# Chunk 0 of a fused state-space and gated-MLP block: all gate steps before all up steps, loads reordered over three queues, a head that goes tile by tile

## The chip, the cores and the metric

The kernel runs on one core of one Trainium2 chip. A core has five instruction streams that run side by side and wait for each other only through semaphores: TensorE (PE, matrix products into the PSUM banks), VectorE (DVE), ScalarE (ACT), GpSimd (POOL) and SyncE (SP, which here only issues transfers). SP, ACT and POOL can issue DMA transfers; each stream works strictly in its own order, so an instruction that waits holds up everything behind it on that engine. The metric is the time of one execution on the device in microseconds (us), lower is better.

## The reference

```python
x  = A_x                       # 1 x 2048 x 448, bf16
xn = layernorm(x)              # mean and variance over the 448 features, eps 1e-5
# branch A: a diagonal complex recurrence with 448 states
Lam_bar = exp(exp(log_dt) * (Lambda_re + 1j*Lambda_im))
Bu      = xn @ (((Lam_bar - 1) / Lam)[:, None] * Bmat).T
h[t]    = Lam_bar * h[t-1] + Bu[t]                 # over 2048 positions
s       = 2 * real(h @ Cmat.T) + xn * Dskip
# branch B: a gated MLP with 1792 hidden units
b       = (sigmoid(xn @ w_gate) * (xn @ w_up)) @ w_down
out     = x + s * silu(b)
```

## The kernel before

**Tiling.** The 2048 positions are 16 tiles of 128 rows, in four chunks of 512 positions. A chunk needs `xnT`, the normalized rows transposed (features on the partitions). Its gate product and its up product each consist of seven steps m = 0 to 6; a step (`gu_mm`, L607 and L608) makes two groups of 128 hidden units for 512 positions with 7 pairs of matmuls on the two halves of the array, into one of three PSUM slots `gu`. ACT or DVE empties the slot (`gu_evac`). In chunk 0 ACT writes tanh of the gate (L622) and DVE combines it with the up slot straight from PSUM into `hF` (L631); in the later chunks ACT empties both slots (L625 with the sigmoid, L635 a copy) and DVE multiplies (L636). The recurrence of a chunk takes `b_units` (PE, L657 to L673), then `ssm_pair` and `ssm_stack` (DVE, the scans at L724 and L756), which leave `hT`. `down` (L785) multiplies `hF` with the third weight `wd`; `yout` (L813) multiplies `hT` with the scaled C matrix and leaves the output tile.

**The order.** Every operation is given to a planner (`Plan`) with an assumed cost, its inputs and its outputs. PE's order is the order of the calls. For the other engines `solve` computes backwards by when an operation is due, then goes forward in time and always takes the ready operation that is due first; `emit` writes the program in that order, engine by engine. From then on the order is fixed. If an assumed cost is too low, an engine meets an instruction whose input isn't there yet and waits with all that stands behind it.

**The head (chunk 0's `xnT`).** For tiles 0 to 3: `stats` (DVE, L347 and L348), `chain` (the reciprocal standard deviation: DVE L358, L359, a power on POOL L361, a reciprocal on DVE L363), `norm` (DVE, L375 and L379), `pe_transpose` (seven PE transposes L404, then a copy on ACT L406 and one on DVE L408). `warm_mm` runs 5 and then 6 idle matmuls (L341). The order on PE is: transposes of tiles 0 and 1, first halves (256 positions) of gate 0 and up 0, transposes of tiles 2 and 3, first half of gate 1, then the second halves of the three. Then `columns` turns four parameter rows into columns (L436 on POOL, L442 on PE), `tables` makes the sine and cosine tables (DVE L476 to L484, ACT L488 to L504) and `coeffs` the coefficients (POOL).

**Later tiles.** For chunks 1 to 3, `chain` runs on POOL alone, two tiles at a time, in six operations (L358, L359, L361, L364, L367, L369), each planned at 0.35 us. `norm` is then on ACT (L382) and `dma_transpose` (L306) makes `xnT` with two transposing transfers per tile from SP.

**The loads.** SP and ACT issue all of them (`load`, L288): the rows of x, the gate and up weights in halves (partitions 0 to 63 and 64 to 127) and blocks of m = 0-1, 2-3, 4-6, the parameter rows, and on ACT at the end `wd` and the last eight tiles of x. The B and C matrices come by transposing transfers on SP (`b_load`, `c_load`).

Of the kernel before, what the change touches and what calls it, by code (L numbers as in the profile page):

```python
# [18 lines left out]
D = 448  # L19
F = 1792  # L20
P = 128
# [51 lines left out]
class Plan:  # L73
# [53 lines left out]
    def solve(self, pe_from):  # L127
# [55 lines left out]
def kernel(  # L183
# [78 lines left out]
    veb, varb = sbt("veb", [NT, 1]), sbt("varb", [NT, 1])  # L262
# [32 lines left out]
    BLK = [(0, 2), (2, 4), (4, 7)]  # L295
# [9 lines left out]
    def tload(keys, o, i, nbytes, r=(), chain=True):  # L305
        add("SP", 1.2, lambda: Q.dma_start_transpose(out=o, in_=i), r=r, w=keys, dma=nbytes * 2, chain=chain)  # L306
# [43 lines left out]
    def chain(t0, n):  # L350
        e, en, c = (V, "DVE", 0.08) if t0 < TPC else (G, "POOL", 0.35)
        ts = range(t0, t0 + n)
        var, mean = mv[:, t0:t0 + n, 1:2], mv[:, t0:t0 + n, 0:1]
        sd, rs, nm = sdb[:, t0:t0 + n, :], rsd[:, t0:t0 + n, :], nmr[:, t0:t0 + n, :]
        ve = veb[:, t0:t0 + n, :]
        bc = lambda t: t[:].unsqueeze(1).to_broadcast((P, n, 1))
        vb = varb[:, t0:t0 + n, :]
        add(en, c, lambda: e.tensor_copy(out=vb, in_=var), r=[("mv", t) for t in ts], w=[("vb", t) for t in ts])  # L358
        add(en, c, lambda: e.tensor_single_scalar(out=ve, in_=vb, scalar=EPS, op=ALU.add),  # L359
            r=[("vb", t) for t in ts], w=[("ve", t) for t in ts])  # L360
        add("POOL", 0.35, lambda: G.tensor_tensor(out=sd, in0=ve, in1=bc(halfc), op=ALU.pow),  # L361
            r=[("ve", t) for t in ts] + ["consts"], w=[("sd", t) for t in ts])
        add(en, c, (lambda: V.reciprocal(out=rs, in_=sd)) if t0 < TPC else  # L363
            (lambda: G.tensor_tensor(out=rs, in0=sd, in1=bc(negc), op=ALU.pow)),  # L364
            r=[("sd", t) for t in ts] + ["consts"], w=[("rs", t) for t in ts])
        if t0 >= TPC:
            add(en, c, lambda: e.tensor_tensor(out=nm, in0=mean, in1=rs, op=ALU.mult),  # L367
                r=[("mv", t) for t in ts] + [("rs", t) for t in ts], w=[("nm", t) for t in ts])
            add(en, c, lambda: e.tensor_single_scalar(out=nm, in_=nm, scalar=-1.0, op=ALU.mult),  # L369
                r=[("nm", t) for t in ts], w=[("nm", t) for t in ts])  # L370

    def norm(t):
        b = t % NXN
        if t < TPC:
            add("DVE", 0.25, lambda: V.tensor_scalar(out=xn[b][:, 0:448], in0=x_all[:, t, :],  # L375
                                                     scalar1=mv[:, t, 0:1], scalar2=rsd[:, t, :],
                                                     op0=ALU.subtract, op1=ALU.mult),
                r=[("x", t), ("mv", t), ("rs", t)], w=[("xn", b)])
            add("DVE", 0.085, lambda: V.tensor_copy(out=xn[b][:, 448:512], in_=xn[b][:, 0:64]),  # L379
                r=[("xn", b)], w=[("xnw", b)])  # L380
        else:
            add("ACT", 0.6, lambda: A.activation(xn[b][:, 0:448], x_all[:, t, :], ACT.Identity,  # L382
# [15 lines left out]
    def pe_transpose(t):  # L398
# [3 lines left out]
        def f():  # L402
# [5 lines left out]
        add("DVE", 0.467, lambda: V.tensor_copy(out=xnT[0][:, 4:7, js], in_=tp[:, 4:7, :]),  # L408
            r=[("acc", a), ("xnT", 0, t, "a")] if False else [("acc", a)], w=[("xnT", 0, t, "b")])

    def dma_transpose(t):
# [4 lines left out]
        tload([k + ("a",)], xnT[c % 3][:, 0:7:2, js], xn[b][:], P * 1024, r=[("xn", b), ("xnw", b)] + al, chain=c == 1)  # L416
        tload([k + ("b",)], xnT[c % 3][:, 1:6:2, js], xn[b][:, 64:448], P * 768, r=[("xn", b)] + al, chain=c == 1)
# [15 lines left out]
    def columns():  # L433
# [28 lines left out]
        for i in range(4):  # L462
# [3 lines left out]
                 ["ident", "pv", "diag"], ["diag"], 0.4)  # L466
# [3 lines left out]
    def tables():  # L470
        turn = C("turn")
        add("ACT", 1.3, lambda: A.preload_act_table_set("silu_and_others"), r=["r", "dt"], w=["silutab"])
        for pt in range(4):
            vk, nk = ("v", pt), ("nu", pt)
            v, nu = v_t[:, pt, :], nu_t[:, pt, :]
            add("DVE", 0.344, lambda v=v, pt=pt: V.tensor_scalar(out=v, in0=iota[:, 0:NTAB], scalar1=turn[:, pt:pt + 1],  # L476
                                                                 scalar2=None, op0=ALU.mult),
                r=[("wv", 0), "turn"], w=[vk])
            add("DVE", 0.344, lambda v=v, nu=nu: V.tensor_single_scalar(out=nu, in_=v, scalar=MAGIC, op=ALU.add),
# [29 lines left out]
        gate([("vrow", q) for q in range(4)] + ["vroww"], [("hF", 1, m) for m in range(7)])  # L509

    def coeffs():
        def ops(o, x, y, op):
            add("POOL", 0.3, lambda: G.tensor_tensor(out=C(o)[:], in0=val(x), in1=val(y), op=op), r=[x, y], w=[o])
# [4 lines left out]
        def one_(o, x, s, op):  # L518
            add("POOL", 0.3, lambda: G.tensor_single_scalar(out=C(o)[:], in_=val(x), scalar=s, op=op), r=[x], w=[o])
# [475 lines left out]
```

## Time and profile before

| | |
|---|---|
| time before, median of 2 runs | 222.81 us (222.48 to 223.13) |
| the profiled execution's own time | 222.76 us |
| its span in the profile | 222.0 us |
| PE busy | 189.1 us (85%) |
| DVE busy | 160.2 us (72%) |
| ACT busy | 112.6 us (51%) |
| POOL busy | 42.6 us (19%) |
| mean granted PE clock | 0.946 |

The span is what the profile shows of one execution; about 0.8 us of the execution's own time lie outside it. Rows of the timeline view give the start, the duration, the engine and source line, output and inputs, how many instructions are merged in the row, and in brackets how long the engine had stood idle before and who released it. "SPq" and "ACTq" are the issues of transfers on those engines. In the view by stretches a row gives a stretch, its length, the busy time of each engine, the granted PE clock as a share of full speed, the busy share of the DMA engines (queued packets overlap, so it can pass 1) and GB/s.

### The profile page before, as it was taken

Reading aid. Unit: us, or ns where it says so; the run is one execution under the profiler, and the core shown is the slowest. Engines: PE = TensorE matmul, PEld = TensorE weight load, DVE = VectorE, ACT = ScalarE, POOL = GpSimd, SP = SyncE. Lnnn points to the kernel's source line nnn. Section 1 sums busy time; section 2 is a strip of 40 time slices with the busy share of each in tenths; the row PEclk is TensorE's granted clock in tenths of the full one; section 3 lists DMA queues with packets and bytes.
Section 4 is the critical chain, followed back from the end, with each engine's and each line's share of the span. In section 5 each row is a group of like instructions: output and inputs, shape, how many; then the busy total and the mean of one; then the engine's idle time right before and its main releaser. Section 6 shows DMA issues by size and latency. Waiting matters only on the chain.

```text
span 222.0 us, 3617 instructions
## 1 busy us (share of the span) xinstructions
PE 189.1 (85%) x1409; PEld 92.5 (42%) x1416; DVE 160.2 (72%) x301; ACT 112.6 (51%) x155; POOL 42.6 (19%) x97
## 2 busy tenths in 40 slices
PE   7200999999899999196999299999999999999993
PEld 2100664344344444043554144444444544455552
DVE  1501677999999999389999688996169799733144
ACT  0004168498999951651952664653655657430330
POOL 4200168621700029500008520000000000000000
PEclk9755699999999999979999769999999999999998
DMA  6999954470000000142001142000000000101002
GB/s 146 213 235 291 355 128 86 84 163 6 1 0 0 3 0 0 25 84 59 1 24 41 28 96 65 0 21 0 24 0 21 3 0 1 44 22 41 3 15 69
DMA packets 30922, 13.32 MB, mean 60 GB/s; under 512 B 19636, under 2 KB 30904, under 8 KB 30904
## 3 DMA queue, kind: packets, MB, share of 16 engines
q1 hardware_dynamic: 25264, 8.95, 17.7%
q10 hardware_dynamic: 5640, 4.13, 7.0%
q8 instruction: 11, 0.18, 0.3%
q14 instruction: 7, 0.06, 0.1%
HBM read 6.66 MB, written 1.84 MB: 38 GB/s over the span
## 4 chain that ended last, share of the span: by engine, by line
PE 47%; DVE 25%; DMA 9%; POOL 8%; ACT 5%; issue 3%; SPq 0%; ACTq 0%; DVEq 0%; POOLq 0%
PE gu L607 17%; PE acc L785 10%; PE acc L813 7%; DMA wG<-in_B_w_gate_dram 5%; PE gu L785 5%; DMA wU<-in_B_w_up_dram 4%; PE gu L670 4%; DVE wv L724 3%; DVE hF L631 3%; POOL sdb L361 2%; POOL rsd L364 2%; DVE bst L347 2%; DVE hF L636 2%; ACT ub L635 2%; DVE hT L741 1%
## 5 line engine op out<-in xcount | busy, mean ns | idle before, releaser
L607 PE MATMUL gu<-xnT,wG 64*128 64x512 bf16 (+1 forms) x210 | 48.1, 367 | 15.4 <-DMA wU<-in_B_w_up_dram 13.0
L607 PE MATMUL gu<-xnT,wU 64*128 64x512 bf16 (+1 forms) x203 | 49.3, 382 | 4.7 <-ACT sig L625 4.7
L608 PE MATMUL gu<-xnT,wU 64*128 64x512 bf16 (+1 forms) x203 | 49.3, 383 | 0.0
L608 PE MATMUL gu<-xnT,wG 64*128 64x512 bf16 (+1 forms) x210 | 48.2, 367 | 0.0
L785 PE MATMUL acc<-wd,hF 128*128 128x448 bf16 x168 | 34.6, 359 | 0.0
L785 PEld LDWEIGHTS <-hF 128*128 128x128 bf16 x224 | 21.8, 99 | 22.4 <-issue 3.6
L607 PEld LDWEIGHTS <-wG 64*128 64x128 bf16 x210 | 19.4, 95 | 24.5 <-issue 4.4
L607 PEld LDWEIGHTS <-wU 64*128 64x128 bf16 x203 | 19.2, 97 | 23.4 <-issue 3.1
L625 ACT ACTIVATE sig<-gu 128x1024 bf16<-128x1024 f32 x21 | 21.5, 1022 | 14.6 <-PE gu L608 14.6
L635 ACT CAST ub<-gu 128x1024 bf16<-128x1024 f32 x21 | 21.2, 1010 | 13.8 <-PE gu L608 13.7
L636 DVE TENSOR_TENSOR hF<-sig,ub 128x1024 bf16<-128x1024 bf16 x21 | 14.3, 682 | 14.9 <-ACT ub L635 14.8
L608 PEld LDWEIGHTS <-wG 64*128 64x128 bf16 x210 | 19.2, 95 | 13.9 <-issue 13.9
L813 PE MATMUL acc<-cT,hT 128*128 128x448 bf16 x105 | 24.3, 353 | 0.0
L724 DVE TENSOR_TENSOR_SCAN wv<-c_r,st,z 128x512 bf16<-128x512 f32 x18 | 22.9, 1280 | 0.2
L608 PEld LDWEIGHTS <-wU 64*128 64x128 bf16 x203 | 19.2, 97 | 5.0 <-issue 5.0
L670 PE MATMUL gu<-xnT,bT 128*128 128x512 bf16 x65 | 16.4, 399 | 1.3 <-issue 1.3
L795 DVE TENSOR_TENSOR g_t<-zb,sigd 128x448 bf16<-128x448 bf16 x16 | 6.2, 384 | 15.1 <-ACT zb L794 15.1
L793 ACT ACTIVATE sigd<-acc 128x448 bf16<-128x448 f32 x12 | 6.5, 541 | 15.1 <-PE acc L785 15.0
L681 ACT CAST bus<-gu 128x1024 bf16<-128x1024 f32 x12 | 12.0, 1006 | 3.9 <-PE gu L670 3.9
L382 ACT ACTIVATE xn<-x_all,nmr,rsd 128x448 bf16<-128x448 bf16 x12 | 8.4, 751 | 10.2 <-POOL nmr L369 10.2
L813 PEld LDWEIGHTS <-hT 128*128 128x128 bf16 x119 | 10.4, 98 | 7.3 <-issue 0.4
L347 DVE BATCH_NORM_STATS2 bst<-x_all 128x6 f32<-128x448 bf16 x16 | 9.4, 612 | 4.6 <-DMA x_all<-in_A_x_dram 4.6
(133 smaller groups left out, 275.9 us busy)
## 6 DMA issues: line engine op xcount, KB each, us to landing
out_dram<-o_t SPq DMA_DIRECT2D x15, 112.0 KB, 1.7
wd<-in_B_w_down_dram ACTq DMA_DIRECT2D x1, 1568.0 KB, 15.5
x_all<-in_A_x_dram ACTq DMA_DIRECT2D x1, 896.0 KB
wG<-in_B_w_gate_dram ACTq DMA_DIRECT2D x2, 224.0 KB, 4.4
wU<-in_B_w_up_dram ACTq DMA_DIRECT2D x2, 224.0 KB, 4.7
wG<-in_B_w_gate_dram SPq DMA_DIRECT2D x2, 224.0 KB, 5.6
wU<-in_B_w_up_dram SPq DMA_DIRECT2D x2, 224.0 KB, 5.9
x_all<-in_A_x_dram SPq DMA_DIRECT2D x1, 448.0 KB, 6.4
```

The lines of the kernel that those rows point to most:

```text
L347: add("DVE", 0.53, lambda: V.bn_stats(out=bst[b][:], in_=x_all[:, t, :]), r=[("x", t)], w=[("bst", b)])
L382: add("ACT", 0.6, lambda: A.activation(xn[b][:, 0:448], x_all[:, t, :], ACT.Identity, bias=nmr[:, t, :], scale=rsd[:, t, :]), r=[("x", t), ...
L607: T.matmul(gu[a][:, 0, ts], lhsT=w_[0:H, s, ms], rhs=x[0:H, s, ts], start=(s == 0), stop=(s == 6))
L608: T.matmul(gu[a][:, 1, ts], lhsT=w_[H:P, (s + 1) % 7, ms], rhs=x[H:P, s, ts], start=(s == 0), stop=(s == 6))
L625: add("ACT", act(1024), lambda: A.activation(sig[b][:], gu[a][:], ACT.Sigmoid), r=[("gu", a), "sinL", "cosL", "sth", "cth"] + [(s, p) for ...
L635: add("ACT", act(1024), lambda: A.copy(out=ub[b][:], in_=gu[a][:]), r=[("gu", a)], w=[("ub", b)])
L636: add("DVE", dve2(1024), lambda: V.tensor_tensor(out=ho, in0=sig[sb_][:], in1=ub[b][:], op=ALU.mult), r=[("sig", sb_), ("ub", b)], w=hk)
L670: T.matmul(gu[a][:, i, :], lhsT=bT[:, kt, i, pt * P:pt * P + P], rhs=x[:, 2 * kt, :], start=False, stop=(kt == 2))
L681: add("ACT", act(1024), lambda u=u, a=a: A.copy(out=bus[u][:], in_=gu[a][:]), r=[("gu", a)], w=[("bus", u)])
L724: dve(1.194, lambda k=k: V.tensor_tensor_scan(out=wv[:, k, :], data0=rb, data1=z[:, k, :], initial=(st[pt][:, k, :] if c else 0.0), op0=AL ...
L785: T.matmul(d, lhsT=hF[c % 2][:, m, h, js], rhs=wd[:, ft, :], start=(ft == 0), stop=(ft == FT - 1))
L813: T.matmul(y, lhsT=hT[c % 2][:, hm, js], rhs=cT[:, cm, c0:c1], start=(i == 0), stop=(i == 6))
```

## The change

**Order of chunk 0.** PE makes all seven gate steps, then all seven up steps; the tanh of gate m waits in `hF` of chunk 1, which is free until then, instead of a ring of two buffers. Ten full steps now precede the two `b_units` of chunk 0 and one follows them; before it was seven and four. The parameter rows move from the memory of the second `hF` to that of the first.

**Loads.** Weight blocks are m = 0-2 and 3-6. SP and ACT load x tiles 0 to 3, then all gate weights, then all up weights; ACT issues only three of these. The parameter rows, `wd` and the last eight tiles of x are issued by POOL. x tiles 4 to 7 come last among SP's plain loads.

**Head.** Each of tiles 0 to 3 has its own chain: DVE adds eps, ACT takes the square root (a table set for it is loaded first), DVE copies the mean and takes the reciprocal. `mv` becomes bf16, so the chains of the later tiles lose one POOL operation. Twelve warm-up matmuls come first. PE's order is: transpose of tile 0, gate steps 0 to 2 for tile 0's 128 positions, transpose of tile 1, the same three steps for tile 1, transposes of tiles 2 and 3, `columns`, then the three steps for tiles 2 and 3.

**Planner.** Its assumed costs change (the POOL operations of a chain from 0.35 to 0.4 or 1.0 us, among others), and an operation that hands over to another engine is due 0.2 us earlier, a transfer 1.5 us instead of 0.5.

```diff
-                if o.dma:
-                    x -= 0.5
+                if kind is not None and o.eng != b.eng:
+                    x -= 1.5 if o.dma else 0.2
...
-    vrow = hF_raw[1][0:1, 0:2048].rearrange("p (a b) -> p a b", a=4)
-    mv = sbt("mv", [NT, 2], FP32)
+    vrow = hF_raw[0][0:1, 0:2048].rearrange("p (a b) -> p a b", a=4)
+    mv = sbt("mv", [NT, 2])
+    meanf = sbt("meanf", [TPC, 1], FP32)
...
-    BLK = [(0, 2), (2, 4), (4, 7)]
+    BLK = [(0, 3), (3, 7)]
...
+    add("ACT", 1.3, lambda: A.preload_act_table_set("sqrt_and_others"), w=["sqrttab"], chain=True)
     load_x(0, 1)
     load_x(1, 1)
+    load_x(2, 2)
     load_w("ACT", "g", 1, 0)
     load_w("SP", "g", 0, 0)
+    load_w("ACT", "g", 1, 1)
+    load_w("SP", "g", 0, 1)
     load_w("ACT", "u", 1, 0)
-    load_x(2, 2)
     load_w("SP", "u", 0, 0)
+    load_w("SP", "u", 1, 1)
+    load_w("SP", "u", 0, 1)
     for k, vec in enumerate((A_log_dt, A_Lambda_im, A_Lambda_re, A_Dskip)):
-        load("ACT", ("vrow", k), D * 2, vrow[:, k, 0:448], vec.unsqueeze(0))
-    for b in (1, 2):
-        if b == 2:
-            load_x(4, 4)
-        for k in ("g", "u"):
-            load_w("SP", k, 0, b)
-            load_w("ACT", k, 1, b)
+        load("POOL", ("vrow", k), D * 2, vrow[:, k, 0:448], vec.unsqueeze(0), cost=1.0)
...
+        if t0 < TPC:
+            add("DVE", 0.09, lambda: V.tensor_single_scalar(out=ve, in_=var, scalar=EPS, op=ALU.add), r=ks("mv"), w=ks("ve"))
+            add("ACT", 0.2, lambda: A.activation(sd, ve, ACT.Sqrt), r=ks("ve") + ["sqrttab"], w=ks("sd"))
+            add("DVE", 0.09, lambda: V.tensor_copy(out=meanf[:, t0:t0 + n, :], in_=mean), r=ks("mv"), w=ks("mf"))
+            add("DVE", 0.09, lambda: V.reciprocal(out=rs, in_=sd), r=ks("sd"), w=ks("rs"))
+            return
...
+        add("POOL", 0.4, lambda: G.tensor_single_scalar(out=ve, in_=var, scalar=EPS, op=ALU.add), r=ks("mv"), w=ks("ve"))
+        add("POOL", 1.0, lambda: G.tensor_tensor(out=sd, in0=ve, in1=bc(halfc), op=ALU.pow), r=ks("ve") + ["consts"], w=ks("sd"))
+        add("POOL", 1.0, lambda: G.tensor_tensor(out=rs, in0=sd, in1=bc(negc), op=ALU.pow), r=ks("sd") + ["consts"], w=ks("rs"))
+        add("POOL", 0.4, lambda: G.tensor_tensor(out=nm, in0=mean, in1=rs, op=ALU.mult), r=ks("mv") + ks("rs"), w=ks("nm"))
+        add("POOL", 0.4, lambda: G.tensor_single_scalar(out=nm, in_=nm, scalar=-1.0, op=ALU.mult), r=ks("nm"), w=ks("nm"))
...
-                add("ACT", act(1024), lambda: A.activation(sig[b][:], gu[a][:], ACT.Tanh, scale=0.5),
-                    r=[("gu", a)], w=[("sig", b)])
+                add("ACT", act(1024), lambda: A.activation(th, gu[a][:], ACT.Tanh, scale=0.5),
+                    r=[("gu", a)], w=[("hF", 1, m)])
...
-        m, k = i // 2, "gu"[i % 2]
+        m, k = (i // 2, "gu"[i % 2]) if c else (i % 7, "gu"[i // 7])
...
-    warm_mm(5)
+    warm_mm(12)
     for t in range(4):
         stats(t)
...
+        chain(t, 1)
+        norm(t)
+    slots0 = [next_gu() for _ in range(3)]
...
     pe_transpose(0)
+    g_head(0, 1)
     pe_transpose(1)
...
+    g_head(1, 2)
     pe_transpose(2)
     pe_transpose(3)
...
     columns()
+    for m in range(3):
+        gu_mm(0, "g", m, slots0[m], 2, 4, m == 0)
+        gu_evac(0, "g", m, slots0[m])
     tables()
     coeffs()
+    load_x(4, 4)
     b_load()
-    load("ACT", "wd", F * D * 2, wd[:], B_w_down.rearrange("(ft p) d -> p ft d", p=P))
-    load_x(8, 8, "ACT")
+    load("POOL", "wd", F * D * 2, wd[:], B_w_down.rearrange("(ft p) d -> p ft d", p=P), cost=1.0)
+    load_x(8, 8, "POOL")
...
-    for i in range(3, 10):
+    for i in range(3, 13):
         gu_step(0, i)
     b_units(0, (0, 1))
     b_units(0, (2, 3))
-    for i in range(10, 14):
-        gu_step(0, i, i == 10)
+    for i in range(13, 14):
+        gu_step(0, i, i == 13)
```

More of the change, by code (lines that the diff above doesn't have):

```diff
@@ L359, in chain @@
[L359 to L370, printed above, removed]
+        sd, rs, nm, ve = (q[:, t0:t0 + n, :] for q in (sdb, rsd, nmr, veb))
+        ks = lambda k: [(k, t) for t in ts]
+        if t0 < TPC:
[4 more added lines that the diff above has]
+            return
@@ L407, in pe_transpose @@
             r=[("acc", a)], w=[("xnT", 0, t, "a")])
[L408 to L409 removed]
+        add("DVE", 0.27, lambda: V.tensor_copy(out=xnT[0][:, 4:7, js], in_=tp[:, 4:7, :]),
+            r=[("acc", a)], w=[("xnT", 0, t, "b")])
     def dma_transpose(t):
```

64 lines of the change are left out of this document (24 added, 40 removed).

## The prediction, made before the changed kernel was run

> **What bounds the kernel now.** I read the page's strip of 40 slices first (5.55 us each), for where PE, which is 85% busy, has holes.
>
> ```profile
> PE   7200999999899999196999299999999999999993
> PEclk9755699999999999979999769999999999999998
> ```
>
> There are three: slices 1 to 3 in the head, slice 16 and its neighbour, slice 22. Elsewhere PE is full, and from slice 23 on it sets the pace to the end. The view by stretches gives each hole its size.
>
> ```profile
> 8.90:21.95 13.05, 0.01 (x1) 0.04 (x1) 0.51 (x3) 2.36 (x3) 0.39 (x1) 0.50 1.14 251
> 53.70:89.80 36.10, 35.24 (x267) 16.19 (x266) 35.45 (x62) 25.98 (x38) 13.43 (x23) 1.00 0.00 1
> 89.80:104.50 14.70, 8.35 (x47) 3.63 (x48) 9.88 (x19) 7.43 (x10) 2.01 (x7) 0.88 0.30 64
> 122.20:131.70 9.50, 5.59 (x18) 2.67 (x19) 6.80 (x11) 7.05 (x10) 4.38 (x9) 0.64 0.27 58
> ```
>
> After the stretch come PE, PEld, DVE, ACT and POOL, the granted clock, the DMA share, GB/s. The head loses 13.0 us. The second hole loses 14.70 - 8.35 = 6.4 us idle, and at a mean clock of 0.88 another 0.12 x 14.70 = 1.8: 8.1 together. The third loses 3.9 idle and, with the 0.36 missing from the clock less a half microsecond that fell on idle time, about 2.9: 6.8. The last two make 14.9 us. Now the causes, from the timeline. First the head:
>
> ```profile
> 8.34 0.57 PE L404 MATMUL acc<-ident,xn 128*128 128x128 bf16 x7 [0.15 <-DVE xn L375]
> 10.83 0.63 ACTq L288 DMA_DIRECT2D wd<-in_B_w_down_dram  x1
> 19.11 0.40 ACTq L288 DMA_DIRECT2D x_all<-in_A_x_dram  x1
> 19.54 1.28 ACT L406 ACT_TABLE_LOAD   x1 [19.54 <-DMA wU<-in_B_w_up_dram]
> 20.83 1.07 ACT L406 COPY xnT<-acc 128x512 bf16<-128x512 bf16 x2
> 21.95 0.37 PE L607 MATMUL gu<-xnT,wG 64*128 64x256 bf16 x1 [13.04 <-DMA wU<-in_B_w_up_dram]
> ```
>
> The bracket on PE names a weight, but the rows above it tell another story: the transposes of tiles 0 and 1 were in PSUM at 8.9, and ACT, which must copy them out, was stuck in its own queue. It issued `wd` at 10.83 and the second half of x only at 19.11, when an up weight had landed; then came its table load, then the copies. PE starts as the second copy ends (21.90). **The head's bound is ACT's queue.** Then the other two holes:
>
> ```profile
> 81.70 0.92 POOL L358 CAST varb<-mv 128x2 bf16<-128x2 f32 x2 [21.55 <-DVE mv L348]
> 90.16 0.79 POOL L369 TENSOR_SCALAR nmr<-nmr 128x2 f32<-128x2 f32 x2
> 90.80 2.71 ACT L382 ACTIVATE xn<-x_all,nmr,rsd 128x448 bf16<-128x448 bf16 x4 [6.18 <-POOL nmr L369]
> 94.47 0.58 PE L607 MATMUL gu<-xnT,wU 64*128 64x512 bf16 x1 [4.70 <-ACT sig L625]
> 102.98 0.37 PE L607 MATMUL gu<-xnT,wG 64*128 64x512 bf16 x1 [1.06 <-DMA xnT<-xn]
> 117.30 0.99 POOL L358 CAST varb<-mv 128x2 bf16<-128x2 f32 x2 [23.49 <-DVE mv L348]
> 123.80 0.41 POOL L369 TENSOR_SCALAR nmr<-nmr 128x2 f32<-128x2 f32 x2
> 124.07 0.76 ACT L382 ACTIVATE xn<-x_all,nmr,rsd 128x448 bf16<-128x448 bf16 x1 [4.07 <-POOL nmr L369]
> 125.78 0.37 PE L660 MATMUL gu<-xnT,bT 64*128 64x256 bf16 x1 [3.60 <-ACT ub L635]
> ```
>
> Both are one mechanism. POOL's chain for two pairs of tiles took 9.2 us (81.70 to 90.95) and 6.9 (117.30 to 124.21); the planner had put it down as 12 x 0.35 = 4.2. ACT meets the norms too early, stands 6.18 and 4.07 us, and behind the norms stand the evacuations that PE waits for.
>
> **The change, part by part. Head.** The rows for its terms:
>
> ```profile
> 0.00:8.90 8.90, 5.66 (x25) 2.33 (x26) 3.83 (x15) 0.00 (x0) 3.48 (x15) 0.99 0.85 174
> 1.30 4.54 PE L341 MATMUL gu<-warm 128*128 128x512 bf16 x11 [1.30 <-POOL warm L309]
> 2.87 0.63 DVE L347 BATCH_NORM_STATS2 bst<-x_all 128x6 f32<-128x448 bf16 x1 [2.87 <-DMA x_all<-in_A_x_dram]
> 21.45 0.85 DVE L408 COPY xnT<-acc 128x384 bf16<-128x384 bf16 x2 [12.41 <-ACT xnT L406]
> 25.06 1.31 PE L404 MATMUL acc<-ident,xn 128*128 128x128 bf16 x14
> 26.01 0.59 ACT L406 COPY xnT<-acc 128x512 bf16<-128x512 bf16 x1 [4.11 <-PE acc L404]
> 27.92 0.27 PE L607 MATMUL gu<-xnT,wG 64*128 64x256 bf16 x1 [0.69 <-ACT xnT L406]
> 28.90 1.02 ACT L622 ACTIVATE sig<-gu 128x1024 bf16<-128x1024 f32 x1 [1.03 <-PE gu L608]
> 29.96 1.22 DVE L631 SCALAR_TENSOR_TENSOR hF<-sig,gu 128x1024 bf16<-128x1024 bf16 x1 [0.92 <-ACT sig L622]
> 30.80 0.39 PE L607 MATMUL gu<-xnT,wU 64*128 64x512 bf16 x1
> ```
>
> Warm-up: 12 x 0.41 from 1.30 ends at 6.3. Tile 0 lands at 2.87; its statistics (0.63) and seven short operations, one of them now on ACT, may take until 6.3 without being seen. The transpose goes at 6.3, and with 0.57, a copy of 0.59 on ACT and 0.43 on DVE behind it `xnT` of tile 0 is there at 7.9. The first gate block needs 448 KB of x and 2 x 336 KB of weights before it: 1.15 MB at the 174 GB/s of the first 8.9 us, 6.6 us, and a good microsecond to complete: 8.0. So gate steps for tile 0 start at **8.0**. Three steps on 128 positions are 21 pairs; the trace has no such matmul. From below: half of a 256-position pair at full clock, 2.3 us for 21 pairs from 27.92 on, so 1.2. From above: that pair at half clock, 0.213 each, 4.5. I take 2.6, since a 128-column transpose with its load takes 0.094 (1.31 for 14) and a pair has two loads. Then 0.57 for the transpose of tile 1, 1.1 for its two copies, 2.6 for the next quarter, 1.31 for the transposes of tiles 2 and 3, 1.4 until their copies are out (`columns`, 16 matmuls of one column, lies in that), and 2.3 for the second halves: 8.0 + 2.6 + 0.57 + 1.1 + 2.6 + 1.31 + 1.4 + 2.3 = 19.9. Ahead of the first tanh ACT must now load another table, because the square root took the first; gate 0 is done at 18.4, 1.28 + 1.02 later its slot is free: first full step at **20.8**, against 30.80. **The head gives 10.0 us** (5 to 13 with both ends of the quarters and a clock that may be low).
>
> [...]
>
> **POOL's transfers.** No POOL issue is in the trace. From below: the same two loads cost ACT 0.63 and 0.40. From above: the 8.7 us that ACT spent between the start of the one and the end of the other. I take 1 us each for all six (nearest: the issue rows). POOL has nothing else before the copy for `columns`, wanted at about 16, so up to 8 us are hidden. `wd` is wanted when PE starts `down`, tens of microseconds later.
>
> **Tiles 4 to 7 load last.**
>
> ```profile
> 13.98 6.80 SPq L306 DMA_TRANSPOSE bT<-in_A_B_re_dram  x2
> 20.83 6.05 SPq L306 DMA_TRANSPOSE bT<-in_A_B_im_dram  x2
> 32.69 10.82 SPq L306 DMA_TRANSPOSE xnT<-xn  x8
> xnT<-xn SPq DMA_TRANSPOSE x24, 2.4
> 41.93 0.39 PE L657 MATMUL gu<-xnT,bT 64*128 64x512 bf16 x1 [0.38 <-DVE bT L552]
> 47.66 0.39 PE L607 MATMUL gu<-xnT,wG 64*128 64x512 bf16 x1
> 53.71 0.38 PE L607 MATMUL gu<-xnT,wG 64*128 64x512 bf16 x1
> ```
>
> Four full steps take 53.71 - 47.66, so 1.51 each, and `b_units` 5.73. Chunk 1 starts at 20.8 + 10 x 1.51 + 5.73 + 1.51 = 43.1 (before: 53.71) and needs all eight transposes, 10.8 us of SP and 2.4 to land. SP carries 2.98 MB up to those tiles, ACT 1.15, and POOL's 2.5 MB share the engines, half or all of them ahead: 5.4 to 6.7 MB. With 1.55 moved by 8.9 us and 251 GB/s after, tiles 4 to 7 land at 24 to 29; statistics (0.63), a pair's chain (half of 6.9, less the dropped cast, 3.0), a norm (0.76) and 13.2 make 42 to 47. So a new wait of 0 to 4 us on PE, with SP's transposes as its cause; I charge **1.0**. The four transposes of B stand on SP between those loads and chunk 1's transposes; issued while the DMA engines were full they held SP 12.9 us (13.98 to 26.88). Now they can follow the last x load from about 10 us on and end at 23 to 28, no later than the tiles are ready, and `b_units` wants them at 36.
>
> **Evacuations.** Ten steps in a row: the gate's tanh 1.02 on ACT, then the up step's 1.22 on DVE, each under 1.51, so three slots suffice. DVE's tables and statistics ahead of the scans are what they were, but six evacuations come before the scans instead of five, 1.22 us more. That has cover:
>
> ```profile
> 76.81 1.39 DVE L585 SCALAR_TENSOR_TENSOR cT<-xnT,c_sa,ctmp 64x448 bf16<-64x448 bf16 x2
> 83.45 0.35 PE L813 MATMUL acc<-cT,hT 128*128 128x448 bf16 x1
> ```
>
> What the first `yout` needs was ready at 78.2, 5.2 us early. Without that cover it would cost the 1.2.
>
> **The two later holes.** The plan now books a pair's chain at 3.2 us, two at 6.4; measured less the dropped cast they would be 8.3 and 5.9. The planner's error falls from 5.0 to 1.9 and from 2.7 to nothing. Taken off PE's idle 4.70 and 3.60 that leaves 1.8 and 0.9, too short to lose the clock (the wait of 1.06 at 103 left it at full), and of 14.9 us some 12 would go. But the whole order is new and DVE, 35.45 of 36.10 busy ahead of the second hole, has no room for statistics that come late. From nothing to 14.9, I take **9.0**.
>
> Sum, on the profiled execution's 222.76: - 10.0 + 1.0 - 9.0 = 204.8, so **205 us**; the median, 222.81, is the same.
>
> **The rivals.** (1) *The holes stay*, because DVE again reaches the statistics late: 222.8 - 9 = 214. For it: it is a new order with the same full DVE. Against: the booked costs. (2) *Both holes close and nothing new waits*: 222.8 - 10 - 14 = 199. (3) *The late tiles bind*: the wait at chunk 1 is 4 to 6 us, PE's clock drops, 1.7 more; with the holes half closed 209, with them open 217. (4) *The change doesn't do what it says*: the first gate steps wait for weights as the bracket at 21.95 says. Then the head gives at most 3 and the time is 211 to 220. Against: 174 GB/s bring the block by 8. [...]
>
> [...]
>
> **How the numbers follow.** Forecast 0.50 (201 to 209), (1) 0.19, (2) 0.12, (3) 0.08, (4) 0.06, (5) 0.05. The range takes in (1), (2) and most of (3): 197 to 216. About 2% is what a measurement here can tell from no change. Faster by more than that: all of 0.50, 0.19, 0.12, 0.07 of (3), 0.03 of (4), together 0.91; within 2%: 0.05; slower: 0.04, the far end of (5).
>
> **What would show it.** In the timeline after: gate matmuls near 8.0 with ACT copies at 7; a full 512-position step near 20.8; chunk 1's first gate step at 43 to 45, and whether a transposing transfer is its releaser; ACT's idle before L382 at 2 us or less and no half-clock stretch past 30 us. The forecast is wrong if POOL is still issuing when `columns` is due, if tiles 4 to 7 land past 29, or if ACT again stands before L382.

## The result and the profile after

The changed kernel takes **206.22 us** (205.85 to 206.59), the kernel before 222.81: a ratio of 0.926 with the interval 0.916 to 0.935. The forecast was 205 (197 to 216). Two kernels among the experiments also had slower executions: one took 208.02 once and 212.65 to 214.11 three times, so it has no ratio and only its head is read, and the last one took 212.45 once in six, which its ratio leaves out.

The strips of the profile after (span 204.8 us, slices of 5.12 us):

```profile
PE   7267995899799999999699999999999999999992
PEclk9859999999999999999999999999999999999998
GB/s 143 235 295 338 223 165 88 74 91 109 89 2 3 0 22 71 78 12 3 73 40 45 48 67 0 3 22 22 0 16 10 0 3 22 22 27 48 0 22 67
```

The clock is at full from slice 3 (15.4 us) to the last but one; before, it fell again in slices 17, 22 and 23. The timeline of PE shows what is left of the holes:

```profile
7.05 0.56 PE L400 MATMUL acc<-ident,xn 128*128 128x128 bf16 x7 [1.18 <-DVE xn L371]
11.68 0.28 PE L603 MATMUL gu<-xnT,wG 64*128 64x128 bf16 x1 [4.07 <-DMA wG<-in_B_w_gate_dram]
15.64 0.21 PE L603 MATMUL gu<-xnT,wG 64*128 64x128 bf16 x1 [0.67 <-ACT xnT L402]
22.03 0.37 PE L603 MATMUL gu<-xnT,wG 64*128 64x512 bf16 x1
33.65 0.37 PE L603 MATMUL gu<-xnT,wU 64*128 64x512 bf16 x1 [2.38 <-ACT hF L619]
41.42 0.37 PE L654 MATMUL gu<-xnT,bT 64*128 64x512 bf16 x1 [1.03 <-DVE hF L628]
48.45 0.38 PE L603 MATMUL gu<-xnT,wG 64*128 64x512 bf16 x1
54.44 0.37 PE L654 MATMUL gu<-xnT,bT 64*128 64x512 bf16 x1 [1.07 <-ACT ub L632]
99.30 0.37 PE L654 MATMUL gu<-xnT,bT 64*128 64x512 bf16 x1 [1.18 <-ACT sig L622]
```

The rows at 11.68, 22.03 and 48.45 are the first gate matmul, the first full step and chunk 1's first gate step; these marks stood at 21.95, 30.80 and 53.71. They cut the gain of 17.2 us of span into three terms: the head to the first full step gives 8.8; from there to chunk 1 takes 26.4 instead of 22.9, a loss of 3.5; from chunk 1 to the end takes 156.4 instead of 168.3, a gain of 11.9.

These terms are good to about 1 us. In the trace after, 1.8 us of the execution's own time lie outside the span (206.59 for 204.8), and 1.7 to 1.8 in every experiment. The 0.8 given for the kernel before doesn't fit that: its trace, of 222.0 us, is then of an execution about 1 us longer than 222.76. The medians differ by 16.6 us, the spans by 17.2.

### The profile page after: what moved, and what is told of

Its sections match the earlier page's. It is cut to its first block, busy times and chain, and to the rows that moved or that the text cites. A ratio compares the mean times of both kernels' runs of the same rounds, so it can differ in the third digit from the quotient of the medians.

```text
span 204.8 us, 3700 instructions
## 1 busy us (share of the span) xinstructions
PE 186.2 (91%) x1459; PEld 92.5 (45%) x1459; DVE 160.0 (78%) x304; ACT 114.6 (56%) x160; POOL 43.4 (21%) x94
## 3 DMA queue, kind: packets, MB, share of 16 engines
q10 hardware_dynamic: 1392, 1.15, 2.6%
## 4 chain that ended last, share of the span: by engine, by line
PE 50%; DVE 23%; DMA 13%; ACT 5%; POOL 4%; issue 2%; SPq 1%; DVEq 0%; POOLq 0%; ACTq 0%
PE gu L603 18%; DMA x_all<-in_A_x_dram 13%; PE acc L782 10%; PE acc L810 8%; PE gu L782 5%; PE gu L667 4%; DVE wv L721 4%; DVE hF L628 3%; DVE bst L347 2%; ACT sig L622 2%; DVE hF L633 2%; DVE cT L572 2%; POOL rsd L364 1%; PE acc L816 1%; POOL sdb L363 1%
## 5 line engine op out<-in xcount | busy, mean ns | idle before, releaser
L603 PE MATMUL gu<-xnT,wG 64*128 64x512 bf16 (+2 forms) x238 | 47.7, 347 | 5.0 <-DMA wG<-in_B_w_gate_dram 4.1
L603 PE MATMUL gu<-xnT,wU 64*128 64x512 bf16 x196 | 46.5, 376 | 2.4 <-ACT hF L619 2.4
L604 PE MATMUL gu<-xnT,wG 64*128 64x512 bf16 (+2 forms) x238 | 47.7, 347 | 0.0
L604 PE MATMUL gu<-xnT,wU 64*128 64x512 bf16 x196 | 46.5, 376 | 0.0
L782 PE MATMUL acc<-wd,hF 128*128 128x448 bf16 x168 | 33.8, 353 | 0.0
L603 PEld LDWEIGHTS <-wG 64*128 64x128 bf16 x238 | 21.4, 98 | 25.4 <-DMA wG<-in_B_w_gate_dram 4.2
L603 PEld LDWEIGHTS <-wU 64*128 64x128 bf16 x196 | 17.9, 94 | 22.8 <-issue 2.1
L604 PEld LDWEIGHTS <-wG 64*128 64x128 bf16 x238 | 21.1, 98 | 1.2 <-issue 1.0
L604 PEld LDWEIGHTS <-wU 64*128 64x128 bf16 x196 | 17.7, 94 | 3.3 <-issue 3.2
L667 PE MATMUL gu<-xnT,bT 128*128 128x512 bf16 x72 | 16.9, 380 | 0.0
L792 DVE TENSOR_TENSOR g_t<-zb,sigd 128x448 bf16<-128x448 bf16 x16 | 6.1, 386 | 12.8 <-ACT zb L791 12.8
## 6 DMA issues: line engine op xcount, KB each, us to landing
wG<-in_B_w_gate_dram SPq DMA_DIRECT2D x1, 448.0 KB, 14.9
```

The costliest lines, as they stand in the source:

```text
L603: T.matmul(gu[a][:, 0, ts], lhsT=w_[0:H, s, ms], rhs=x[0:H, s, ts], start=(s == 0), stop=(s == 6))
L604: T.matmul(gu[a][:, 1, ts], lhsT=w_[H:P, (s + 1) % 7, ms], rhs=x[H:P, s, ts], start=(s == 0), stop=(s == 6))
L667: T.matmul(gu[a][:, i, :], lhsT=bT[:, kt, i, pt * P:pt * P + P], rhs=x[:, 2 * kt, :], start=False, stop=(kt == 2))
L782: T.matmul(d, lhsT=hF[c % 2][:, m, h, js], rhs=wd[:, ft, :], start=(ft == 0), stop=(ft == FT - 1))
```

## The experiments

The experiments' times are medians of four to six executions; the kernel before had 222.65 to 223.07 beside them. The last three columns come from the timelines of the profiled executions, one for each kernel.

| kernel | us | ratio, interval | first gate matmul | chunk 1 starts | chunk 1 to end |
|---|---|---|---|---|---|
| before | 222.81 | | 21.95 | 53.71 | 168.3 |
| after | 206.22 | 0.926, 0.916-0.935 | 11.68 | 48.45 | 156.4 |
| before, planner's numbers | 217.59 | 0.975, 0.970-0.981 | 22.40 | 53.89 | 161.8 |
| before, two loads on POOL | 210.13 | 0.940, 0.934-0.947 | 14.96 | 50.08 | 159.3 |
| before, both of these | 205.01 | 0.918, 0.912-0.923 | 15.01 | 47.81 | 155.3 |
| after without both | 208.0 to 214.1 | | 15.27 | - | - |
| after, old planner's numbers | 208.51 | 0.934, 0.929-0.940 | 11.70 | 48.72 | 157.3 |
| after, gate and up alternate | 206.27 | 0.922, 0.915-0.928 | 12.09 | 47.93 | 156.0 |

**The planner's numbers alone, in the kernel before.**

```diff
-                if o.dma:
-                    x -= 0.5
+                if kind is not None and o.eng != b.eng:
+                    x -= 1.5 if o.dma else 0.2
...
-        e, en, c = (V, "DVE", 0.08) if t0 < TPC else (G, "POOL", 0.35)
+        e, en, c = (V, "DVE", 0.08) if t0 < TPC else (G, "POOL", 0.4)
+        cp = 0.35 if t0 < TPC else 1.0      # price of both pow operations
```

> The kernel before with only the planner's numbers of the change: the later due times (0.2 us a hand-over, 1.5 us a transfer) and 0.4 / 1.0 us for POOL's chain operations. If the planner's numbers close the two later holes (theory A), the head stays as it is (first gate matmul near 22 us) and ACT no longer stands before L382: time 209 to 213 us. If the holes close because the new head gives the engines other phases (theory B), the holes stay and the time is 219 to 224 us.

217.59, between the two forecasts. The head is as before, and by the spans 6.5 us of the rest are gone (the medians give 5.3 for the whole). ACT's waits ahead of the norms shrink as the prediction said (6.18 and 4.07 before), but PE now waits for chunk 2's transposes, with the clock at half from 99.4 to 106.3 (rows of ACT, SP and PE):

```profile
90.26 2.71 ACT L383 ACTIVATE xn<-x_all,nmr,rsd 128x448 bf16<-128x448 bf16 x4 [1.94 <-POOL nmr L370]
123.57 1.41 ACT L383 ACTIVATE xn<-x_all,nmr,rsd 128x448 bf16<-128x448 bf16 x2 [1.69 <-POOL nmr L370]
98.85 2.56 SPq L306 DMA_TRANSPOSE xnT<-xn  x2
101.62 0.58 PE L608 MATMUL gu<-xnT,wG 64*128 64x512 bf16 x1 [5.61 <-DMA xnT<-xn]
```

So the planner's numbers (margins and prices were not run apart) are a cause of the two holes, but not enough of one. The chain takes 7.5 us instead of 9.2, but the last of the statistics it needs (tile 11) ends at 83.1 instead of 81.2, so it ends at 90.81 where it ended at 90.95, and SP has the eight transposes behind it until 101.4.

**The two bulk loads alone, issued by POOL, in the kernel before.**

```diff
-    load("ACT", "wd", ...)
-    load_x(8, 8, "ACT")
+    load("POOL", "wd", ..., cost=1.0)
+    load_x(8, 8, "POOL")
```

> The kernel before with only the third weight and the last eight tiles of x issued by POOL instead of ACT. If ACT's blocked queue is what bounds the head (theory A), the copies of tiles 0 and 1 come at 9 to 10 us instead of 20.8 and the first gate matmul at 10 to 13; the head gives 5 to 9 us and, with the holes as they are, the time is 214 to 218 us. If the loads themselves bound the head (theory B), the first gate matmul comes after 18 us and the time is 219 to 223 us.

210.13, from two changed lines, and less than either forecast. The timeline of ACT and PE in the head:

```profile
12.54 1.28 ACT L406 ACT_TABLE_LOAD   x1 [12.54 <-issue]
13.83 1.07 ACT L406 COPY xnT<-acc 128x512 bf16<-128x512 bf16 x2
14.96 0.37 PE L607 MATMUL gu<-xnT,wG 64*128 64x256 bf16 x1 [5.46 <-ACT xnT L406]
```

ACT comes to its copies 7.0 us earlier (13.83 against 20.83), and PE starts as the second copy ends. That the bound of the head is ACT's queue is shown by this, though not at once freed: the copies were expected at 9 to 10 us, and ten issues still hold ACT until 12.51. What had not been expected: with the planner's old prices the later part shrinks by 9.0 us as well. The planner places work by when it believes a load lands; with other loads ahead it finds another order, in which ACT norms tiles 8 to 11 in two pairs, the first at 82.69, where it did all four at 90.80. ACT still stands 4.73 us ahead of them, but PE waits 1.40 where it waited 4.70 (ACT, PE):

```profile
82.69 1.41 ACT L382 ACTIVATE xn<-x_all,nmr,rsd 128x448 bf16<-128x448 bf16 x2 [4.73 <-POOL nmr L369]
87.21 0.37 PE L607 MATMUL gu<-xnT,wU 64*128 64x512 bf16 x1 [1.40 <-ACT sig L625]
```

**Both together in the kernel before.** Of the title only the third queue is in this kernel: gate and up alternate, the other loads keep their order and the head its pairs.

> The kernel before with two edits together that were run one at a time: the two bulk loads issued by GpSimd instead of ScalarE (alone 12.8 us), and the planner's new margins and GpSimd prices (alone 5.3 us). The gate steps still alternate with the up steps, the head still works by pairs of tiles, the loads keep their old order. Theory A: the two gains are of different holes and add up: 204 to 207 us, so that the gate-first order and the per-tile head buy next to nothing of the 16.6 us. Theory B: they close the same holes: 208 to 211 us, and 2 to 4 us of the change are left for the order of the steps and the head.

205.01, as fast as the whole change within the noise. The strip of its page shows a later and deeper gap in the head and otherwise the same picture:

```profile
PE   7409989899898999999899999999999999999992
28.89 1.65 DVE L347 BATCH_NORM_STATS2 bst<-x_all 128x6 f32<-128x448 bf16 x3
60.94 1.42 ACT L383 ACTIVATE xn<-x_all,nmr,rsd 128x448 bf16<-128x448 bf16 x2
```

The statistics of tiles 8 to 11 are done by 32 us, in time that DVE has to spare, and all their norms by 62.4. The two gains, 5.3 and 12.8 alone, are 18 together, so they add up.

**What the rest of the change does alone.** The changed kernel with the two loads back on ACT and the planner's old numbers:

```diff
-    load("POOL", "wd", ..., cost=1.0)
-    load_x(8, 8, "POOL")
+    load("ACT", "wd", ...)
+    load_x(8, 8, "ACT")
...
-                if kind is not None and o.eng != b.eng:
-                    x -= 1.5 if o.dma else 0.2
+                if o.dma:
+                    x -= 0.5
...
+    # the five prices of the chain on POOL: 0.35 each
```

> The changed kernel without the two edits that together took the kernel before to 205.01 us: the down weights and tiles 8 to 15 are issued by ScalarE again, and the planner has its old margin and GpSimd prices. What is left of the change is the gate-first order, the new order of the weight loads (three of them on ScalarE instead of six), the small vectors on GpSimd and the per-tile head. Theory A: the new load order by itself keeps ScalarE's queue short, so that its two bulk loads are issued by 5 us and its copies of the head aren't late: first gate matmul at 11 to 13 us, 206 to 210 us. Theory B: ScalarE still stands in front of one of the bulk loads until weights have landed, with its square roots and copies behind it: first gate matmul at 16 us or later, 213 to 219 us.

208.0 to 214.1, unsettled between the two. The head shows the mechanism of Theory B in a milder form (rows of ACT's queue, of ACT and of PE):

```profile
12.35 0.38 ACTq L289 DMA_DIRECT2D x_all<-in_A_x_dram  x1
12.77 0.20 ACT L357 ACTIVATE sdb<-veb 128x1 bf16<-128x1 bf16 x1 [10.77 <-DMA wG<-in_B_w_gate_dram]
13.66 0.93 PE L400 MATMUL acc<-ident,xn 128*128 128x128 bf16 x7 [7.06 <-DVE xn L371]
```

With five loads instead of twelve ACT is free at 12.8 instead of 19.5. The shorter queue is thus a second way to the head's gain, and the parts of the change replace one another: without both edits the rest still takes 9 to 15 us off, while the two alone take 18.

**The planner's numbers in the new order.** The second and third part of that edit, in the changed kernel:

> The changed kernel with the old planner margin (0.5 us for transfers only) and 0.35 us for all POOL chain operations. Theory A (the planner's numbers close the holes): ACT stands 3 to 6 us before L382 again, holes of 2 to 5 us at chunks 2 and 3, time 212 to 217 us. Theory B (the new head closes them): no hole, time 205 to 208 us.

208.51, between the two forecasts: worth some 2.3 us by the medians (the intervals overlap) and 1.2 between the profiled executions, against 5.3 in the old order. ACT does stand before the norms again, as Theory A said, but PE's longest wait behind the head is 2.88 us, at 98.01 (ACT, PE):

```profile
96.29 0.76 ACT L378 ACTIVATE xn<-x_all,nmr,rsd 128x448 bf16<-128x448 bf16 x1 [6.30 <-POOL nmr L366]
98.01 0.37 PE L603 MATMUL gu<-xnT,wU 64*128 64x512 bf16 x1 [2.88 <-ACT sig L622]
```

**Gate-first undone.** Behind the first three gate steps chunk 0 goes up 0, gate 3, up 1 and so on to gate 6, then the last three up steps; all else is the changed kernel's.

```diff
-        m, k = (i // 2, "gu"[i % 2]) if c else (i % 7, "gu"[i // 7])
+        # chunk 0, i = 0..13: g0 g1 g2 u0 g3 u1 g4 u2 g5 u3 g6 u4 u5 u6
```

> The changed kernel with only the order of chunk 0's steps undone behind the first three gate steps: up 0, gate 3, up 1, gate 4 and so on to gate 6, then the last three up steps. Loads, head and planner stay. Theory A: gate-first matters because the up weights land late (their first block near 24 us): up 0 follows the three gate steps at about 22, waits 2 us or more, and the time is 208 to 211 us. Theory B: the order of the steps is worth nothing by itself once the loads are issued early, since VectorE also gets its first evacuation sooner and the tanh waits at 33.65 us go: 205 to 207 us.

206.27 against 206.22. Up 0 does wait for its weights, 0.81 us at 23.29, and other waits go in return. **Behind the first three steps, the order named in the title is worth nothing that shows.**

**Why is the first gate matmul late?** First, POOL's two bulk loads put behind the table arguments, so that they are issued at 23.36 and 26.14 us:

```diff
-    load("POOL", "wd", ..., cost=1.0)
-    load_x(8, 8, "POOL")
+    load("POOL", "wd", ..., cost=1.0, r=["arg"])
+    load_x(8, 8, "POOL", r=["arg"])
```

> The changed kernel, with GpSimd's two bulk loads (the down weights and tiles 8 to 15 of x, 2.4 MB) put behind the table arguments in GpSimd's order instead of at 4.6 and 11.6 us. Theory A: in the head these loads share the DMA engines with the gate and up weights and with tiles 4 to 7, and that is what keeps the first gate matmul at 11.68 us (forecast 8.0) and tiles 4 to 7 at 28.8. Then the first gate matmul starts at 9 to 10.5, tiles 4 to 7 land at 22 to 24, the waits of 2.38 and 1.03 us before chunk 1 go, and the time is 201 to 204 us. Theory B: the gate weights are late because of the up weights and x on the other two queues; first gate matmul at 11 to 12, and the late loads now meet the transposes of chunk 1 instead: 206 to 209 us.

206.05 (0.921, 0.915-0.927). The first gate matmul is at 11.61, so these loads don't hold it. They do hold SP's up weights and tiles 4 to 7, which take 11 us from issue to landing here and 19 in the changed kernel: the waits of 2.38 and 1.03 are gone and chunk 1 starts at 45.68, 2.8 earlier. From there to the end it takes 157.8 instead of 156.4, and the clock falls (PE's timeline, then the view by stretches, with the clock behind the five busy times):

```profile
94.91 0.37 PE L654 MATMUL gu<-xnT,bT 64*128 64x512 bf16 x1 [1.26 <-ACT ub L632]
96.48 0.58 PE L654 MATMUL gu<-xnT,bT 64*128 64x512 bf16 x1 [1.18 <-ACT sig L622]
96.20:99.60 3.40, 2.79 (x8) 1.02 (x9) 3.37 (x8) 2.37 (x4) 0.08 (x1) 0.51 0.35 74
```

Second, the first gate block ahead of tiles 2 and 3 on SP's queue, tiles 4 to 7 early, and eight more warming matmuls behind the first transposes:

```diff
     load_x(1, 1)
-    load_x(2, 2)
     load_w("ACT", "g", 1, 0)
     load_w("SP", "g", 0, 0)
+    load_x(2, 2)
...
     pe_transpose(0)
+    warm_mm(8)
     g_head(0, 1)
...
+    # and the two edits of tiles 4 to 7, below
```

> The changed kernel with tiles 4 to 7 early and their statistics behind the columns (205.35 us), the first block of gate weights ahead of tiles 2 and 3 on SyncE's queue, and eight more warming matmuls behind the first transposes. Theory A: the first gate matmul is late because 448 KB of x stand ahead of SyncE's half of the gate weights; it now starts at 9.5 to 10.5 us, at full clock, tiles 2 and 3 come about 2 us later but still before they are needed, and the time is 202 to 204 us. Theory B: tiles 2 and 3 now are what the head waits for: first full step at 22 to 23 us as before, 204.5 to 206 us.

208.73 (0.936, 0.931-0.940), slower than the 205.35 us kernel it is made from and outside both forecasts, but it answers the question (PE, ACT, PE):

```profile
9.73 0.23 PE L604 MATMUL gu<-xnT,wG 64*128 64x128 bf16 x1
13.13 0.20 ACT L358 ACTIVATE sdb<-veb 128x1 bf16<-128x1 bf16 x1 [4.52 <-DVE veb L357]
14.18 0.57 ACT L403 COPY xnT<-acc 128x512 bf16<-128x512 bf16 x1
14.80 0.21 PE L604 MATMUL gu<-xnT,wG 64*128 64x128 bf16 x1 [3.22 <-ACT xnT L403]
```

The gate matmuls now follow the warming ones without a wait, at 9.73 and at full clock (1.00 granted from 9.65 to 11.05), where the 205.35 us kernel has them at 11.40. Of the 448 KB of x ahead of SP's half of the weights only tiles 2 and 3 have moved, so these 224 KB were the cause. But tile 2 now lands at 12.06, ACT's square root for it stands before the copy of tile 1, and PE waits there. Against the 205.35 us kernel the first full step still comes 1.65 earlier, at 22.83, but chunk 1 starts 1.13 later, at 47.97, and from there to the end it takes 158.6 instead of 157.5.

**Tiles 4 to 7 earlier.** Their load ahead of the up weights on SP:

```diff
+    load_x(4, 4)
     load_w("ACT", "u", 1, 0)
     load_w("SP", "u", 0, 0)
...
-    load_x(4, 4)
     b_load()
```

> The changed kernel with x tiles 4 to 7 issued on SP ahead of the up weights instead of behind them. If the late tiles are what holds DVE at 28.8 us and PE at 33.6 and 41.4 (theory A), those waits of 2.4 and 1.0 us go and the time is 202 to 204 us. If the up weights then come late (theory B), PE waits for them at about 29 us instead and the time is 205 to 208 us.

211.33 (0.947, 0.940-0.953), five slower than the change and slower than either forecast. They landed at 23.11 instead of 28.82, but the planner had put their statistics ahead of the copies of tiles 2 and 3 (DVE's timeline):

```profile
23.11 0.63 DVE L348 BATCH_NORM_STATS2 bst<-x_all 128x6 f32<-128x448 bf16 x1 [5.37 <-DMA x_all<-in_A_x_dram]
23.66 0.60 DVE L405 COPY xnT<-acc 128x384 bf16<-128x384 bf16 x2
```

The same with these statistics ordered behind the table columns:

```diff
-            r=[("x", t)], w=[("bst", b)])
+            r=[("x", t)] + (["pv"] if t in (4, 5, 6, 7) else []), w=[("bst", b)])
...
+    # veb of these tiles on POOL reads "arg" as well
```

> The changed kernel with tiles 4 to 7 loaded ahead of the up weights, as in the run that took 211.33 us, but with their statistics on VectorE ordered behind the copy of the table columns, and their chains on GpSimd behind the table arguments. Theory A: that run lost its time because VectorE stood 5.37 us for these tiles with the copies of tiles 2 and 3 behind it. Then the first full gate step is back at 22 to 23 us, TensorE doesn't wait 2.7 us for the columns, and the time is 203 to 206 us. Theory B: the loss came from the up weights (later on the same queue) or from the gate weights waiting behind x: first gate matmul again near 13.4, first full step at 25 or later, 208 to 212 us.

205.35 (0.917, 0.910-0.925): the diagnosis holds, 6 us lie in this order. The first full step was expected at 22 to 23 and is at 24.48, since PE ran at half clock until 23.9 (matmuls of 256 columns take 0.42 us before that and 0.27 behind it); chunk 1 still starts at 46.84, and a new wait of 2.32 comes at 53.85.

**A version that beats both?** The 205.01 us kernel with the four small vectors on POOL too, which leaves six loads on ACT:

```diff
-        load("ACT", ("vrow", k), D * 2, vrow[:, k, 0:448], vec.unsqueeze(0))
+        load("POOL", ("vrow", k), D * 2, vrow[:, k, 0:448], vec.unsqueeze(0), cost=1.0)
```

> The kernel before with the two bulk loads on GpSimd and the planner's new numbers (205.01 us), and the four small vectors on GpSimd too, so that ScalarE issues six weight loads and nothing else. Theory A: what still holds ScalarE until 12.6 us is the number of loads ahead of its table load (ten); with six it comes to its copies at 8 to 10 us, the first gate matmul starts at 10.5 to 12.5 instead of 15.01, and the time is 201 to 204 us, below the changed kernel. Theory B: the last weight loads wait for something else, or the gate weights themselves land no earlier than 14: first gate matmul at 14 to 15, 204 to 206 us.

210.69 (0.946, 0.942-0.951), slower than either forecast. The head did as hoped: table load at 9.81, first gate matmul at 12.23. The loss comes 77 us later (PE, ACT, DVE):

```profile
93.44 0.37 PE L608 MATMUL gu<-xnT,wG 64*128 64x512 bf16 x1 [3.87 <-DMA xnT<-xn]
82.11 2.72 ACT L383 ACTIVATE xn<-x_all,nmr,rsd 128x448 bf16<-128x448 bf16 x4 [0.22 <-POOL nmr L370]
74.18 1.65 DVE L347 BATCH_NORM_STATS2 bst<-x_all 128x6 f32<-128x448 bf16 x3
```

The statistics of tiles 9 to 11 are back at 74 us, due by the planner's prices. Swapping the two loads on POOL's queue, x first, should bring them forward:

```diff
+    load_x(8, 8, "POOL")
     load("POOL", "wd", ..., cost=1.0)
-    load_x(8, 8, "POOL")
```

> The kernel of the 210.69 us run (the kernel before with bulk loads and small vectors on GpSimd and the planner's new numbers), with the two bulk loads swapped on GpSimd's queue: tiles 8 to 15 of x first, the down weights second. Theory A: that run started its gate steps 2.8 us earlier than the 205.01 us kernel and gave it back at 89.57 us, where TensorE waited 3.87 us for chunk 2's transposes, because the planner had put the statistics of tiles 9 to 11 just in time at 74 us by its prices, where in the 205.01 us kernel they fell into VectorE's early idle time. With tiles 8 to 15 believed to land earlier the statistics go early again: no wait over 1.5 us at 85 to 95, first gate matmul still at 12 to 12.5, and the time is 200.5 to 203.5 us. Theory B: the start doesn't pass through, since other rows become late in its place (the copies of the B matrix, the first evacuations on VectorE): 204 to 207 us whatever the order of the loads.

204.91 (0.921, 0.917-0.924). The mechanism of Theory A is confirmed: the statistics of tiles 4 to 14 lie between 19.7 and 30 us, and nothing waits at 85 to 95. Its time was not reached: the head starts 2.9 us before that of the 205.01 us kernel, chunk 1 1.1, and the rest gives that back (waits of 1.65 at 34.32 for the copy of B and 1.16 at 53.09 among it), as Theory B said of the start. Against the changed kernel (206.22) neither it nor the 205.01 us kernel can be called faster, since the intervals overlap.

## Why the prediction was right, and where it was not

**Gate steps at 8.0: wrong, 11.68.** The sum let the block's own 1.15 MB have the whole rate; its good microsecond to complete was the author's estimate, and no run shows it apart. By the rates of the strip 1.9 MB moved in the first two slices (143 and 235 GB/s for 5.12 us each), while ACT's second gate block and up weights were in flight too and SP's half stood behind x in its own queue. Moving that half ahead of tiles 2 and 3 (9.73) showed it.

**Quarter steps 2.6 each: near for the first by luck, 1.2 too long for the second.** The view by stretches has the two quarters, the first at half clock; the row of PE is the transposes of tiles 2 and 3:

```profile
11.68:14.00 2.32, 2.32 (x42) 2.16 (x42) 1.52 (x6) 0.07 (x1) 1.30 (x2) 0.50 1.01 317
15.64:17.09 1.45, 1.45 (x43) 1.21 (x42) 0.34 (x1) 0.00 (x0) 0.00 (x0) 1.00 1.04 342
17.09 0.96 PE L400 MATMUL acc<-ident,xn 128*128 128x128 bf16 x14
```

At full clock a quarter took 1.45, which is 0.069 for each of its 21 pairs. That is what one transpose takes at this clock (0.96 for 14), where the sum counted two for a pair; its 0.094 was measured at a mean clock of 0.70 (25.00 to 26.40 in the kernel before). The first quarter came near 2.6 only because PE, idle for 4.07 us before it, ran it at half clock. Tiles 2 and 3 were there when the second quarter ended. So of the 3.7 us of the late start only 1.2 arrive at the first full step, 22.03 for 20.8: the second quarter gives back 1.2 and the table some 0.9. **The head: 8.8 for 10.0.**

**The table: right in size, not in place.** The sum put the load behind gate 0. ACT loaded it at 19.56 for the exponential of the first column, while PE was in gate 0 until 20.5, so that the first full step comes 1.5 us behind gate 0 where the sum had 2.4. The load took 1.28 us, and in ACT's timeline that exponential starts 0.02 us behind it:

```profile
19.56 1.28 ACT L443 ACT_TABLE_LOAD   x1
20.86 0.20 ACT L443 ACTIVATE c_dt<-pv 128x4 bf16<-128x4 f32 x1
```

**POOL's issues at 1 us: right, rival (5) falls.** The four small ones took 0.49 to 0.76, the large ones:

```profile
4.62 1.16 POOL L289 DMA_DIRECT2D wd<-in_B_w_down_dram  x1
11.61 0.89 POOL L289 DMA_DIRECT2D x_all<-in_A_x_dram  x1
```

That is 0.65 and 0.87 ns a row (1792 and 1024 rows). POOL's copy for `columns` starts at 11.12, behind 5.34 us in which POOL waited for a parameter row to land and not for an issue, and its last issue ends at 12.50. The 0.05 given to (5), by which issues on POOL hold up the head, rested on a price for each row that was the author's assumption; no run shows it.

**Late tiles: the landing right, the term too small and in another place, 3.5 for 1.0.** The rows of DVE and ACT:

```profile
28.82 1.15 DVE L347 BATCH_NORM_STATS2 bst<-x_all 128x6 f32<-128x448 bf16 x2 [4.07 <-DMA x_all<-in_A_x_dram]
32.06 0.63 ACT L484 ACTIVATE spm<-hT 128x512 bf16<-128x512 f32 x1 [4.00 <-DVE hT L477]
```

They landed inside the forecast's 24 to 29, if only just, and SP's transposes were in time at chunk 1, which started at 48.45 and not at 43 to 45. But DVE stood 4.07 us for them with the tables behind, ACT's sine stood 4.00 for the tables with a tanh behind, and PE lost 2.38 and then 1.03. The prediction had followed the tiles to the transposes and not asked what was queued behind their statistics. The kernel with late bulk loads, in which DVE doesn't wait for these tiles, showed it.

**The later holes: 11.9 for 9.0, with the wrong main cause.** ACT's idle time ahead of the norms is down as foreseen, at 2.36 just past the 2 us that were set, and no stretch of chunks 1 to 3 is at half clock up to 202.9 us:

```profile
80.19 1.41 ACT L378 ACTIVATE xn<-x_all,nmr,rsd 128x448 bf16<-128x448 bf16 x2 [1.72 <-POOL nmr L366]
96.02 0.76 ACT L378 ACTIVATE xn<-x_all,nmr,rsd 128x448 bf16<-128x448 bf16 x1 [2.36 <-POOL nmr L366]
```

But the planner's numbers gave 6.5 of the rest when alone, the two moved loads 9.0 without them, and in the new order the numbers were worth 0.9 of it. The step that failed is the one that took the fall of the planner's error off PE's idle time, one for one. ACT's wait and PE's loss don't go together like that: ACT stood 4.73 and PE lost 1.40 with the moved loads and old prices, 6.30 and 2.88 in the new order with old prices, 1.94 and 5.61 with the new numbers alone. What the sum left out is where the planner puts the statistics of tiles 8 to 15, and so when their loads are believed to land: swapping two loads brought the statistics of tiles 9 to 11 from 74 us to before 30 and the time from 210.69 to 204.91. How much of the 11.9 in the changed kernel belongs to which edit can't be said, since they replace one another.

Two sums of the working are also off, without consequence. What is left of 4.70 is 1.6, not 1.8, when the error falls by 3.1. Rival (3) leaves out the 1.7 us of clock that it names: with a wait of 5 us its times are 210.5 and 219.5.

So the time came within 1.2 us with terms off by 1.2 and 2.5 to one side and 2.9 to the other. The queue that bound the head and the direction of every term were foreseen; that the sum came so close is luck. Rivals (1) to (3) and (5) fell. (4) was half true: the first gate steps do wait 4.07 for weights, and 1.2 of it reached the first full step.

## What to carry to other kernels

Before crediting a rewrite to what it is named after, run its smallest parts alone: here two load lines and four of the planner's numbers give the whole gain, and the order of the later steps gives none that shows. A bulk load on a compute engine's queue can cost what stands behind it there (ACT's copies came 7.0 us earlier once two such loads were on POOL's), so put it on an engine that has nothing to do, and on each queue put what is needed first in front. Where an order is planned from prices, an earlier start can come back as a wait 77 us later; read the term "from the next chunk to the end" beside the head for each version.

## What the runs showed of the hardware

In these traces an engine that issued a load on a queue with loads in flight was at times held for microseconds. On SP's queue in the changed kernel the longest hold in a plain load, 8.39 us, is in one issue, that of tiles 4 to 7:

```profile
9.63 8.39 SPq L289 DMA_DIRECT2D x_all<-in_A_x_dram  x1
```

It ends at 18.02, when the second gate block of the same queue, issued near 3.0 and 14.9 us under way, has just landed. That the issue waits for such a landing is a reading of this one coincidence and was not tested. The same load took 0.39 in the kernel before. ACT, with two bulk loads behind three weight loads (the change without both edits), stood from 2.9 to 12.4 us but for the 0.40 of one issue. No issue of POOL's in any of the kernels took longer than 1.33 us, but POOL never issued more than two bulk loads.

The half-clock stretches that end inside the span come in whole multiples of 3.41 us in the traces before and after: two (6.83 us) at the start of the changed kernel, and five, one and two (17.07, 3.41 and 6.83 us) in the kernel before, where they also start a whole number of such windows apart: at 8.77, 94.10 and 124.82 us, so 25 and 34 windows behind the first. The row 96.20 to 99.60 above, at 0.51, fits one. The rows are the changed kernel twice and the kernel with the ordered statistics:

```profile
8.40:15.20 6.80, 3.28 (x49) 2.92 (x50) 4.37 (x18) 0.61 (x3) 1.76 (x3) 0.50 1.08 277
32.30:35.70 3.40, 2.04 (x18) 0.99 (x19) 3.40 (x7) 3.37 (x7) 3.07 (x7) 1.00 0.17 37
51.20:54.60 3.40, 0.72 (x6) 0.14 (x3) 2.86 (x6) 3.37 (x6) 3.06 (x8) 1.00 0.00 0
```

What a wait cost here hung on where it fell among these windows. The 2.38 us before 33.65 in the changed kernel lie across two windows (28.9 to 32.3 and 32.3 to 35.7), PE is busy for 2.39 and 2.04 us of them, and both they and the next are at full clock. The 2.32 us before 53.85 with the ordered statistics lie inside one, PE is busy for 0.72 us of it, and in the next window, from 54.6 on, the matmuls of 512 columns take 0.58 us where those before the wait took 0.38. Cut into such windows up to 200 us, the traces before and after have five at full clock with PE busy for 1.46 us or less (1.46, 0.00 and 0.77 before, 1.45 and 1.28 after), each followed by half clock, and none with 1.65 us or more (1.65 from 97.14 on after) that was. That this is a rule wasn't shown. The head of the kernel before with the planner's numbers looks different: with a mean granted clock of 0.984 for the whole trace the clock's record has room for some 6.9 us at half, which those from 99.4 to 106.3 take up, and so for none in the 13 us of idle time; but the first matmuls of 256 columns then take 0.41 us, as at half clock in the kernel before (0.42), and not 0.27.
